# Statistics in the third buffer of scaled scores, and the value products of tiles 12 and 13 ahead of the first wo part, behind an attention loop

## The chip, the cores and the metric

The kernel runs on one core of a Trainium2 chip. The metric is device time in microseconds (us), the median of several executions. The engines are named as in the profile: PE multiplies matrices (PEld is its weight load), DVE, ACT and POOL do elementwise work, and SP issues DMA transfers. POOL also issues some.

## The reference, cut to what matters

One block: an adaptive layer norm, attention against a cached K and V, a second adaptive layer norm, and a mixer with an MLP. Everything is bf16 at the edges; x has 2048 rows of D = 640, there are 32 heads of 128, and 2048 cached keys.

```python
mod = (silu(c) @ w_mod).reshape(...)          # sa, ca, ga, sb, cb, gb
h = layernorm(x) * (1 + ca) + sa
q = (h @ wq)                                  # 32 heads of 128
p = softmax(q @ k_cache.T * 128 ** -0.5)
x = x + ga * ((p @ v_cache) @ wo)
h = layernorm(x) * (1 + cb) + sb
y = gelu(layernorm(h) @ w1)                   # quarters of its columns shifted by +1, -1, +2, -2 rows
x1 = h + shifted(y) @ w2
x = x + gb * (x1 + gelu(layernorm(x1) @ w3) @ w4)
```

So each row passes three more statistics (mean and variance over 640 columns) behind the attention: of x (level 0), of h (level 1) and of x1 (level 2).

## The kernel before

The rows are cut into NQT = 16 tiles of 128. The attention loop runs over NG = 512 steps s (head h, tile j). In a step, PE makes the scores (`qk`, L295), DVE scales them into one of three buffers of `negS` (buffer s % 3) and takes the row minimum (L583), ACT makes the exponentials into a ring (`Pb`, L596), and these are transposed, mostly by DMA (L226) and for some tiles on PE (`t_piece`, L257, with a copy out of the bank by ACT, L266, or DVE, L268). Some 8 to 11 steps later PE makes the value products (`pv`, L308) into two banks `O`; ACT copies a pair of tiles out (`of_copy`, L535); and POOL normalizes a group of four tiles (`rcp` L449, `norm` L456) into one of two halves of `On` and issues the store of that group to a scratch in DRAM (`o_scratch`, L463).

Behind the loop the order is written out by hand (L744 to L768). Left over from the loop are the last eight tiles of the last head: tiles 8 to 11 (steps NG - 8 to NG - 5), which were transposed by DMA, and tiles 12 to 15, which PE transposes (`t_all`). `pv2(g)` makes the value products of two tiles and their copy, and `norm4` normalizes and stores a group: 124 to 127 are the groups of tiles 0 to 3, 4 to 7, 8 to 11 and 12 to 15 of the last head.

`a_part(j, h0, h1, parts)` (L647) is the product of tile j's outputs with wo, for some heads and some columns (NC2: 512 and 128). It accumulates in one of two banks of `Sps`, (j + 1) % 2. Its outputs come transposed from `o_scratch`: `load_ot0` (L509) brings tiles 0 and 1, first 31 heads and then the last, into `hTx`; `load_ot(pr)` (L504) brings tiles 2 pr and 2 pr + 1, for odd pr into the first part of `negS` and for even pr into `hTx`. `load_xt` (L515) brings x. w1 (L769) and w2 (L770) are loaded behind all value products; w2 lies in `negS`, after the part that the outputs use.

In the loop over tiles from L773 on, `a_pe(i)` is tile i's wo product (tiles 0 and 1 are already made), `a_s1(i)` the gate, the sum with x (L659, L661) and the statistics of level 0, and `a_s2(i - 1)` the second norm (L667, L670) and the statistics of level 1. Then `nrm_of` (L682) and a transposing DMA `n_t` (L688) make the input of the mixer.

Statistics are in `stats_of`: two `bn_stats` (L635) and a `bn_aggr` (L637) on DVE; `rs_of` then makes (variance + eps) ** -0.5 on POOL (L628, L630), with the exponent from a small tile `mhalf`, which one memset (L771) fills. Before, all these small tiles lie over `On`, so L635 and the memset wait until `On` is free (ONK: every key of `On`).

Engines run their own instructions in program order; `Prog` puts a semaphore wait in front of an instruction for each key that it reads or writes and that another engine or a DMA wrote or read before.

Of the kernel before, what the change touches and what calls it, by code (L numbers as in the profile page):

```python
# [8 lines left out]
F32 = mybir.dt.float32  # L9
# [106 lines left out]
def bass_adaLN_cond__mha_block_cached__mixer_s_mlp__prompt_kernel(  # L116
    nc, A_x, A_k_cache, A_v_cache, A_wq, A_wo, B_x, B_w1, B_w2, B_w3, B_w4, c, w_mod, out,
):
    _, SQ, D = A_x.shape
    _, H, SK, DH = A_k_cache.shape  # L120
    FF = B_w3.shape[1]
    assert DH == 128 and D % 128 == 0 and SQ % 512 == 0 and SK == 2048
    KT = D // 128
# [8 lines left out]
    NG = H * NQT  # L132
# [5 lines left out]
    with ExitStack() as es:  # L138
# [11 lines left out]
        if True:  # L150
            with ExitStack() as es1:
# [7 lines left out]
                negS = sb1("negS", [128, 3, SK], F32)  # L159
# [5 lines left out]
                On = sb1("On", [128, 2, 4, 128], BF16)  # L165
# [35 lines left out]
                G = Prog(nc, es1, "a")  # L201
# [49 lines left out]
                def t_piece(g, r, q):  # L251
                    jb = bank(("t", g, r))

                    def f(t):
                        for z in range(4 * q, 4 * q + 4):
                            kt = 8 * r + z
                            ins = t.transpose(JBb[jb][:, z * 128:(z + 1) * 128], Pb[:, g % RPB, kt * 128:(kt + 1) * 128], ident[:])  # L257
                        return ins
                    G.op("tensor", f, r=[("Pb", g % RPB)], w=[("J", jb)])

                def t_evac(g, r):
                    jb = bank(("t", g, r))
                    dst = PTs[:, g % RPT, r * 8:(r + 1) * 8, :]
                    src = JBb[jb].rearrange("p (k q) -> p k q", k=8)
                    if not by_dve(g, r):
                        G.op("scalar", lambda a: a.copy(dst, src), r=[("J", jb)], w=[("PT", g % RPT, r)])  # L266
                    else:
                        G.op("vector", lambda v: v.tensor_copy(dst, src), r=[("J", jb)], w=[("PT", g % RPT, r)])  # L268
# [72 lines left out]
                if H > 1:  # L341
# [8 lines left out]
                     r=["id0"], w=["ident"])  # L350
# [3 lines left out]
                for k in range(KT):  # L354
                    G.op("gpsimd", lambda g, k=k: g.tensor_scalar(out=s_bc[:, k, :], in0=ones_f, scalar1=c_f[:, k:k + 1],
                                                                  scalar2=1.0, op0=ALU.mult, op1=ALU.mult),
                         r=["onesf", "cf"] + WRK, w=[("sbc", k)])
# [89 lines left out]
                def rcp(gr):  # L447
                    b = gr % 2
                    G.op("gpsimd", lambda g: g.tensor_tensor(  # L449
                        out=rl[:, 4 * b:4 * b + 4], in0=Of[:].rearrange("p a z d -> p (a z) d")[:, 4 * b:4 * b + 4, 128],  # L450
                        in1=mone, op=ALU.pow),
                         r=[("Of", 2 * b), ("Of", 2 * b + 1), "mone"], w=[("rl", b)])

                def norm(gr, z):
                    b = gr % 2
                    G.op("gpsimd", lambda g: g.tensor_scalar(  # L456
                        out=On[:, b, z, :], in0=Of[:, 2 * b + z // 2, z % 2, 0:128],
                        scalar1=rl[:, 4 * b + z:4 * b + z + 1], scalar2=1.0, op0=ALU.mult, op1=ALU.mult),
                        r=[("Of", 2 * b + z // 2), ("rl", b)], w=[("On", b, z)])
                    if z < 3:  # L460
                        return
                    hh, jj = divmod(4 * gr, NQT)
                    G.dma("gpsimd", lambda e: e.dma_start(  # L463
                        o_scr[jj // 2:jj // 2 + 2, :, hh].rearrange("a p z d -> p a (z d)"),
                        On[:, b].rearrange("p (a z) d -> p a (z d)", a=2)),
                        ("o", b), r=[("On", b, z) for z in range(4)], w=[("os", b), ("osd", jj // 4, hh)])
# [9 lines left out]
                negb = negS[:].rearrange("p r s -> p (r s)").bitcast(BF16)  # L476
# [10 lines left out]
                w4 = wof[:, KT * FF:KT * FF + NFT * D].rearrange("p (f n) -> p f n", f=NFT)  # L487
                ob = wof[:, KT * FF + NFT * D:KT * FF + (NFT + 2) * D].rearrange("p (b d) -> p b d", b=2)
                nrm = Of[:].rearrange("p a z d -> p (a z d)").bitcast(BF16)[:, 0:3 * D].rearrange("p (b d) -> p b d", b=3)
                sm = On[:].rearrange("p a z d -> p (a z d)").bitcast(F32)  # L490
                stt = sm[:, 0:NQT * 12].rearrange("p (t z) -> p t z", t=NQT)
                mvt = sm[:, 192:192 + 3 * NQT * 2].rearrange("p (l t z) -> p l t z", l=3, t=NQT)
                rst = sm[:, 288:288 + 3 * NQT].rearrange("p (l t) -> p l t", l=3)
# [1 line left out]
                mhalf = sm[:, 384:385]  # L495
# [4 lines left out]
                ONK = [("On", b, z) for b in range(2) for z in range(4)]  # L500
# [7 lines left out]
                def load_ot0(h0, h1):  # L508
                    G.dma("sync", lambda e: e.dma_start_transpose(  # L509
                        OTj[0][:, 2 * h0:2 * h1, :], o_scr[0, :, h0:h1].rearrange("q h z d -> q (h z d)")),  # L510
                        ("ot0", h0), r=[("osd", 0, hh) for hh in range(h0, h1)],
                        w=[("OT", 0)] + HTK if h0 == 0 else [("OTB", 0)])
# [9 lines left out]
                for g in range(NG - 8):  # L522
                    d = max(PVE, min(PVD, PVE + (NG - 12 - g) // 2))
# [15 lines left out]
                def norm4(gr):  # L539
                    rcp(gr)  # L540
                    for z in range(4):
                        norm(gr, z)

                for s in range(NG):
                    h, j = divmod(s, NQT)
# [5 lines left out]
                    if s == 3:  # L551
                        G.op("gpsimd", lambda g: g.tensor_scalar(
                            out=mod_bc[:, 2 * D:3 * D], in0=mod_bc[:, 2 * D:3 * D], scalar1=1.0, scalar2=1.0, op0=ALU.add, op1=ALU.mult),
                            r=[("mod", i) for i in range(len(MROW))], w=["mod"])
# [25 lines left out]
                    for half in range(2):  # L580
                        if s < NG:
# [6 lines left out]
                                r=[("S", half)], w=[("negS", s % 3), ("nmh", half, r8)])  # L588
# [3 lines left out]
                    if s < NG:  # L592
                        G.op("gpsimd", lambda g, r8=r8: g.tensor_scalar(  # L593
                            out=nm[:, r8:r8 + 1], in0=nm0[:, r8:r8 + 1], scalar1=nm1[:, r8:r8 + 1], scalar2=None, op0=ALU.min),
                            r=[("nmh", 0, r8), ("nmh", 1, r8)], w=[("nm", r8)])
                        G.op("scalar", lambda a, s=s, r8=r8: a.activation(  # L596
                            Pb[:, s % RPB, :], negS[:, s % 3, :], ACT.Exp, bias=nm[:, r8:r8 + 1], scale=-1.0),
                            r=[("negS", s % 3), ("nm", r8)], w=[("Pb", s % RPB)])
# [13 lines left out]
                    for g_ in NORMS.get(s, []):  # L612
                        gr, z = divmod(g_, 4)
# [13 lines left out]
                def rs_of(l, j):  # L627
                    G.op("gpsimd", lambda g: g.tensor_scalar(out=vet[:, l, j:j + 1], in0=mvt[:, l, j, 1:2], scalar1=float(EPS), scalar2=1.0,  # L628
                                                             op0=ALU.add, op1=ALU.mult), r=[("mvt", l, j)], w=[("vet", l, j)])
                    G.op("gpsimd", lambda g: g.tensor_tensor(out=rst[:, l, j:j + 1], in0=vet[:, l, j:j + 1], in1=mhalf, op=ALU.pow),  # L630
                         r=[("vet", l, j), "mhalf"], w=[("rst", l, j)])

                def stats_of(l, j, src, key):
                    for z in range(2):
                        G.op("vector", lambda v, z=z: v.bn_stats(stt[:, j, 6 * z:6 * z + 6], src[:, z * HD:(z + 1) * HD]),  # L635
                             r=[key], w=[("stt", j, z)] + ONK)
                    G.op("vector", lambda v: v.bn_aggr(mvt[:, l, j], stt[:, j, :]), r=[("stt", j, 0), ("stt", j, 1)], w=[("mvt", l, j)])  # L637
                    rs_of(l, j)

                def a_part(j, h0, h1, parts):  # L640
                    b = (j + 1) % 2
                    pr, z = divmod(j, 2)

                    def f(t):
                        for c0, cw in parts:
                            for hh in range(h0, h1):
                                ins = t.matmul(YB[b][:, c0:c0 + cw], OTj[pr % 2][:, 2 * hh + z, :], wo[:, hh, c0:c0 + cw],  # L647
                                               start=(hh == 0), stop=(hh == H - 1))
                        return ins
                    G.op("tensor", f, r=[("OTB", 0) if pr == 0 and h0 == H - 1 else ("OT", pr % 2)] + WOK, w=[("S", b)])  # L650
# [42 lines left out]
                for n in range(KT):  # L693
                    lst = []
                    p = 0
                    while p < 128:
# [8 lines left out]
                        p = pe_  # L705
# [27 lines left out]
                def t_all(g, r):  # L733
                    for q in range(2):
                        t_piece(g, r, q)
                    t_evac(g, r)

                def pv2(g):
                    for g_ in (g, g + 1):
                        for half in range(2):  # L740
                            pv(g_, half)
                    of_copy(g // 2)

                for g in (NG - 4, NG - 3):  # L744
                    for r in range(2):
                        t_all(g, r)
                norm4(H * 4 - 3)
                load_ot0(H - 1, H)
                a_part(0, 0, H // 2, NC2[0:1])
                for r in range(2):  # L750
                    t_all(NG - 2, r)
                a_part(0, H // 2, H - 1, NC2[0:1])
                for r in range(2):
                    t_all(NG - 1, r)
                pv2(NG - 4)
                a_part(0, 0, H - 1, NC2[1:2])
                pv2(NG - 2)
                norm4(H * 4 - 1)
# [9 lines left out]
                norm4(H * 4 - 2)  # L768
                G.dma("sync", lambda e: e.dma_start(w1, B_w1.rearrange("(k p) n -> p k n", p=128)), "w1", w=["w1"] + KVK)  # L769
                G.dma("sync", lambda e: e.dma_start(w2, B_w2.rearrange("(k p) n -> p k n", p=128)), "w2", w=["w2"] + NEG)  # L770
                G.op("gpsimd", lambda g: g.memset(mhalf, -0.5), w=["mhalf"] + ONK)  # L771

                for i in range(NQT + 1):  # L773
                    if i < NQT:
# [114 lines left out]
                for op_, in1, r_ in ((ALU.mult, mod_bc[:, 3 * D:4 * D], ["mod"]), (ALU.add, xt[:, NQT - 1], [("x1", NQT - 1)])):  # L889
                    G.op("gpsimd", lambda g, op_=op_, in1=in1: g.tensor_tensor(out=xb[:, NQT - 1], in0=xb[:, NQT - 1], in1=in1, op=op_),  # L890
                         r=r_ + [("xb", NQT - 1)], w=[("xb", NQT - 1), ("xg", NQT - 1)])
# [31 lines left out]
```

## Time and profile before

| | |
|---|---|
| time, median of 3 runs | 1604.11 us (1598.97 to 1604.65) |
| the profiled execution | 1605.5 us, span 1603.7 us |
| mean granted clock of PE | 0.994 |
| PE busy | 1511.8 us, 94% |
| DVE busy | 1397.1 us, 87% |
| ACT busy | 1269.4 us, 79% |
| POOL busy | 626.3 us, 39% |
| end of the last exponential | 1269.5 us |
| first wo part (L647) starts | 1270.1 us |
| last matmul of the wo products ends | 1428.9 us |

Times in what follows are us from the start of the span. The span is the profiled execution from its first to its last instruction; 1.8 us of the execution lie around it. A list of waits gives the engine, its line and who released it, and idle time in a timeline stands in square brackets. Everything up to about 1267 us is the same instructions before and after the change.

### The profile page before, as it was taken

Reading aid. Unit: us, or ns where it says so; the run is one execution under the profiler, and the core shown is the slowest. Engines: PE = TensorE matmul, PEld = TensorE weight load, DVE = VectorE, ACT = ScalarE, POOL = GpSimd, SP = SyncE. Lnnn points to the kernel's source line nnn. Section 1 sums busy time; section 2 is a strip of 40 time slices with the busy share of each in tenths; the row PEclk is TensorE's granted clock in tenths of the full one; section 3 lists DMA queues with packets and bytes.
Section 4 is the critical chain, followed back from the end, with each engine's and each line's share of the span. In section 5 each row is a group of like instructions: output and inputs, shape, how many; then the busy total and the mean of one; then the engine's idle time right before and its main releaser. Section 6 shows DMA issues by size and latency. Waiting matters only on the chain.

```text
span 1603.7 us, 34871 instructions
## 1 busy us (share of the span) xinstructions
PE 1511.8 (94%) x14119; PEld 956.1 (60%) x14119; DVE 1397.1 (87%) x2466; ACT 1269.4 (79%) x1114; POOL 626.3 (39%) x1396
## 2 busy tenths in 40 slices
PE   5899999999999999999999999999999889999999
PEld 3466666666666666666666666666666655554444
DVE  6999999999999999999999999999999637667424
ACT  4999999999999999999999999999999600034230
POOL 0144444444444444444444444444444433332100
PEclk9999999999999999999999999999999999999999
DMA  9999999999999999999999999999999987815100
GB/s 296 241 228 234 233 247 237 247 233 232 241 228 238 237 229 234 243 237 240 247 249 234 236 228 242 234 238 232 235 232 239 238 199 145 159 31 152 38 17 34
DMA packets 1183073, 337.27 MB, mean 210 GB/s; under 512 B 1163648, under 2 KB 1176896, under 8 KB 1182912
## 3 DMA queue, kind: packets, MB, share of 16 engines
q1 hardware_dynamic: 1176768, 318.26, 101.9%
q0 software_dynamic: 6144, 16.79, 3.1%
q8 instruction: 111, 1.82, 0.5%
q14 instruction: 50, 0.41, 0.1%
HBM read 43.48 MB, written 19.40 MB: 39 GB/s over the span
## 4 chain that ended last, share of the span: by engine, by line
ACT 32%; PE 21%; DMA 21%; DVE 17%; issue 8%; POOL 0%; ACTq 0%; DVEq 0%; POOLq 0%
ACT ring L596 26%; DMA ring<-ring 19%; DVE negS L583 15%; PE Sps L647 8%; PE Sps L845 4%; ACT ring L266 2%; ACT Of L535 2%; PE Oaug L829 2%; PE QPp L829 2%; ACT kv L248 1%; PE Sps L811 1%; PE PTp L308 1%; DVE ring L373 1%; PE Sps L295 1%; DMA hTx<-o_scratch 1%
## 5 line engine op out<-in xcount | busy, mean ns | idle before, releaser
L583 DVE TENSOR_SCALAR_CACHE_REDUCE negS<-Sps 128x1024 f32<-128x1024 f32 x1024 | 1179.2, 1221 | 35.8 <-PE Sps L295 17.7
L596 ACT ACTIVATE ring<-negS,small 128x2048 bf16<-128x2048 f32 x512 | 1008.4, 2019 | 37.9 <-DMA ring<-ring 29.7
L308 PEld LDWEIGHTS PTp<-kv,ring 128*128 128x128 bf16 x8192 | 558.8, 98 | 238.6 <-DMA ring<-ring 1.4
L295 PE MATMUL Sps<-kv 128*128 128x512 bf16 x2048 | 618.3, 384 | 50.5 <-DVE negS L583 42.8
L308 PE MATMUL PTp<-kv,ring 128*128 128x129 bf16 x8192 | 644.1, 220 | 0.4 <-DMA ring<-ring 0.4
L593 POOL TENSOR_SCALAR small<-small 128x1 f32<-128x1 f32 x512 | 145.9, 285 | 632.8 <-DVE negS L583 632.5
L295 PEld LDWEIGHTS Sps<-kv 128*128 128x128 bf16 x2048 | 125.9, 97 | 198.5 <-DVE negS L583 164.5
L456 POOL TENSOR_SCALAR On<-Of,small 128x128 bf16<-128x128 f32 x512 | 189.8, 371 | 13.2 <-DMA o_scratch<-On 0.3
L449 POOL TENSOR_TENSOR small<-Of,small 128x4 f32<-128x4 f32 x128 | 133.2, 1040 | 26.3 <-ACT Of L535 26.1
L241 PE MATMUL Oaug<-hTx,kv 128*128 128x512 bf16 x320 | 122.1, 386 | 11.2 <-ACT ring L266 8.3
L241 PE MATMUL QPp<-hTx,kv 128*128 128x512 bf16 x320 | 120.5, 381 | 2.6 <-ACT hTx L400 2.0
L463 POOL DMA_DIRECT2D o_scratch<-On x128 | 103.1, 806 | 40.8 <-POOL On L456 37.2
L535 ACT COPY Of<-PTp 128x259 f32<-128x259 f32 x256 | 97.1, 379 | 16.0 <-PE PTp L308 16.0
L727 ACT ACT_TABLE_LOAD x1 | 1.3, 1283 | 112.3 <-POOL hTx L778 112.3
L583 DVE DVE_READ_ACCUMULATOR negS<-Sps 128x1 f32 x1024 | 85.9, 84 | 0.0
L647 PE MATMUL Sps<-wo,negS 128*128 128x128 bf16 (+1 forms) x512 | 73.0, 305 | 5.4 <-DVE ring L659 5.4
L647 PE MATMUL Sps<-wo,hTx 128*128 128x512 bf16 (+1 forms) x512 | 70.7, 299 | 2.4 <-DMA hTx<-o_scratch 2.4
L628 POOL TENSOR_SCALAR On<-On 128x1 f32<-128x1 f32 x48 | 24.6, 512 | 118.2 <-DVE On L637 118.2
L862 DVE TENSOR_TENSOR ring<-Sps,ring 128x640 f32<-128x640 f32 x15 | 12.4, 824 | 65.5 <-PE Sps L845 65.5
L266 ACT COPY ring<-Oaug 128x1024 bf16<-128x1024 bf16 x64 | 65.5, 1024 | 4.7 <-PE Oaug L257 4.7
L647 PEld LDWEIGHTS Sps<-wo,negS 128*128 128x128 bf16 x512 | 40.2, 99 | 37.8 <-DVE ring L659 5.6
L647 PEld LDWEIGHTS Sps<-wo,hTx 128*128 128x128 bf16 x512 | 39.4, 98 | 32.2 <-DMA hTx<-o_scratch 2.6
(84 smaller groups left out, 975.5 us busy)
## 6 DMA issues: line engine op xcount, KB each, us to landing
kv<-in_A_v_cache_dram SPq DMA_DIRECT2D x32, 512.0 KB, 5.0
o_scratch<-On POOLq DMA_DIRECT2D x128, 128.0 KB, 5.2
ring<-in_A_x_dram SPq DMA_DIRECT2D x8, 640.0 KB, 6.0
kv<-in_A_wq_dram SPq DMA_DIRECT2D x32, 160.0 KB, 3.8
wo<-in_A_wo_dram SPq DMA_DIRECT2D x1, 5120.0 KB, 16.9
ring<-ring SPq DMA_TRANSPOSE x254, 7.2
ring<-in_w_mod_dram SPq DMA_DIRECT2D x1, 3200.0 KB, 14.2
out_dram<-wo SPq DMA_DIRECT2D x16, 160.0 KB, 1.8
```

The source lines that it names most:

```text
L241: G.op("tensor", lambda t: t.matmul(JB[jb], wq[:, hb, q, :], hT[:, q, cc * 512:(cc + 1) * 512], start=(q == 0), stop=(q == KT - 1)), r=[(" ...
L266: G.op("scalar", lambda a: a.copy(dst, src), r=[("J", jb)], w=[("PT", g % RPT, r)])
L295: ins = t.matmul(Sps[:, col:col + 512], QT[:, hb, j * 128:(j + 1) * 128], KTs[:, hb, col:col + 512], start=True, stop=True)
L308: ins = t.matmul(ob[:, 0:129], PTs[:, b, kt, :], Vaug[:, hb, kt, 0:129], start=(kt == 0), stop=(kt == NKT - 1))
L449: G.op("gpsimd", lambda g: g.tensor_tensor(out=rl[:, 4 * b:4 * b + 4], in0=Of[:].rearrange("p a z d -> p (a z) d")[:, 4 * b:4 * b + 4, 128 ...
L456: G.op("gpsimd", lambda g: g.tensor_scalar(out=On[:, b, z, :], in0=Of[:, 2 * b + z // 2, z % 2, 0:128], scalar1=rl[:, 4 * b + z:4 * b + z ...
L463: G.dma("gpsimd", lambda e: e.dma_start(o_scr[jj // 2:jj // 2 + 2, :, hh].rearrange("a p z d -> p a (z d)"), On[:, b].rearrange("p (a z) d ...
L535: G.op("scalar", lambda a: a.copy(Of[:, p % 4].rearrange("p z d -> p (z d)")[:, 0:259], PO[:, (p % 2) * 512:(p % 2) * 512 + 259]), r=[("O" ...
L583: G.op("vector", lambda v, half=half, s=s, r8=r8: v.tensor_scalar(out=negS[:, s % 3, half * 1024:(half + 1) * 1024], in0=Sps[:, half * 102 ...
L593: G.op("gpsimd", lambda g, r8=r8: g.tensor_scalar(out=nm[:, r8:r8 + 1], in0=nm0[:, r8:r8 + 1], scalar1=nm1[:, r8:r8 + 1], scalar2=None, op ...
L596: G.op("scalar", lambda a, s=s, r8=r8: a.activation(Pb[:, s % RPB, :], negS[:, s % 3, :], ACT.Exp, bias=nm[:, r8:r8 + 1], scale=-1.0), r=[ ...
L647: ins = t.matmul(YB[b][:, c0:c0 + cw], OTj[pr % 2][:, 2 * hh + z, :], wo[:, hh, c0:c0 + cw], start=(hh == 0), stop=(hh == H - 1))
```

## The change

The statistics' tiles move from `On` to the end of the third buffer of `negS`, after the part where w2 goes (elements 11392 to 12162 of 12288 in bf16). `bn_stats` now depends on `mhalf` and no longer on `On`; the memset of `mhalf` is placed ahead of `norm4` of group 125 and waits for the third buffer of `negS`. In the order behind the loop, the transposes of tile 14 and the value products of tiles 12 and 13 (`pv2(NG - 4)`) come ahead of the first wo part, and the transposes of tile 15 ahead of the second.

```diff
-                sm = On[:].rearrange("p a z d -> p (a z d)").bitcast(F32)
+                SM0 = 2 * H * 128 + KT * D
+                assert 2 * SK * 2 <= SM0 and SM0 + 770 <= 6 * SK
+                sm = negb[:, SM0:SM0 + 770].bitcast(F32)
...
                         G.op("vector", lambda v, z=z: v.bn_stats(stt[:, j, 6 * z:6 * z + 6], src[:, z * HD:(z + 1) * HD]),
-                             r=[key], w=[("stt", j, z)] + ONK)
+                             r=[key, "mhalf"], w=[("stt", j, z)])
...
                 for g in (NG - 4, NG - 3):
                     for r in range(2):
                         t_all(g, r)
+                G.op("gpsimd", lambda g: g.memset(mhalf, -0.5), w=["mhalf", ("negS", 2)])
                 norm4(H * 4 - 3)
                 load_ot0(H - 1, H)
+                for r in range(2):
+                    t_all(NG - 2, r)
+                pv2(NG - 4)
                 a_part(0, 0, H // 2, NC2[0:1])
                 for r in range(2):
-                    t_all(NG - 2, r)
+                    t_all(NG - 1, r)
                 a_part(0, H // 2, H - 1, NC2[0:1])
-                for r in range(2):
-                    t_all(NG - 1, r)
-                pv2(NG - 4)
                 a_part(0, 0, H - 1, NC2[1:2])
                 pv2(NG - 2)
                 norm4(H * 4 - 1)
...
                 G.dma("sync", lambda e: e.dma_start(w2, B_w2.rearrange("(k p) n -> p k n", p=128)), "w2", w=["w2"] + NEG)
-                G.op("gpsimd", lambda g: g.memset(mhalf, -0.5), w=["mhalf"] + ONK)
```

Behind these lines, unchanged: `load_xt(0)`, `load_ot(1)`, `load_xt(1)` to `load_xt(3)`, the wo product of tile 1 and the last head of tiles 0 and 1, `pv2(NG - 8)`, `pv2(NG - 6)` (tiles 8 to 11), `norm4` of group 126, and the loads of w1 and w2.

## The prediction

> **What bounds the kernel now.** I read the page first: PE is busy for 1511.8 of 1603.7 us, and the change touches only what follows the attention loop, so only gaps of PE behind the loop can pay. The list of waits between 1255 and 1332 us (engine, line, waited for: total, times, longest) names them:
>
> ```profile
> DVE On L635 <- POOL On L771: 14.5, 1, 14.5
> POOL On L771 <- DMA o_scratch<-On: 7.9, 1, 7.9
> PE Sps L647 <- DVE ring L659: 5.4, 1, 5.4
> PE Sps L647 <- DMA hTx<-o_scratch: 2.4, 1, 2.4
> ```
>
> PE has two gaps: 2.4 us before the first wo part, which waits for a load of outputs, and 5.4 us later, where DVE has yet to empty a bank of scores. The chain of waits (start us, us, what) shows what stands behind the second:
>
> ```profile
> 1284.24 8.96 PE Sps L647 x66
> 1293.20 3.75 PE PTp L308 x64
> ...
> 1300.29 8.66 DMA o_scratch<-On
> ...
> 1309.00 0.10 POOL On L771
> ...
> 1309.20 0.90 DVE On L635 x2
> ...
> 1310.33 0.70 DVE ring L659
> ```
>
> The statistics of tile 0 (L635) are written over the outputs' buffer On, so they wait until group 126 has been stored from it; the multiply of tile 1 (L659), queued behind them on DVE, frees the bank that PE wants for tile 3. Next, the timeline of PE and the stretches around the gap (us, us; busy time and count for PE, PEld, DVE, ACT, POOL; granted clock, DMA share, GB/s):
>
> ```profile
> 1311.07 11.30 PE L647 MATMUL Sps<-wo,negS 128*128 128x512 bf16 x64 [5.43 <-DVE ring L659]
> ```
>
> ```profile
> 1268.00:1272.00 4.00, 1.89 (x9) 0.90 (x10) 0.48 (x1) 1.54 (x1) 2.99 (x6) 1.00 1.25 274
> 1312.00:1314.00 2.00, 2.00 (x6) 0.66 (x5) 1.93 (x5) 0.00 (x0) 0.79 (x2) 0.50 1.07 242
> 1314.00:1316.00 2.00, 2.00 (x6) 0.76 (x5) 1.93 (x5) 0.00 (x0) 1.17 (x2) 0.50 0.00 0
> ```
>
> After the 5.4 us gap the granted clock is 0.50 until about 1316, and tile 3's 64 matmuls take 11.30 us. Tile 4 starts at 1322.21, 11.14 us after tile 3; undisturbed, the chain gives 8.69 us for 64 of them (at 1420.15). So the gap costs another 2.45 us. After the 2.4 us gap the clock stays 1.00. Last, what comes in next:
>
> ```profile
> 1296.97 0.37 SPq L769 DMA_DIRECT2D kv<-in_B_w_dram  x1
> 1297.39 0.53 SPq L770 DMA_DIRECT2D negS<-in_B_w_dram  x1
> 1297.96 14.19 SPq L504 DMA_TRANSPOSE hTx<-o_scratch  x1
> ```
>
> This L504 brings the outputs of tiles 4 and 5. The rows of L504 give 11.1/11.5/16.3 us to landing (least, median, most), and the look at its own issue gives it the 16.3: it lands at 1314.26. PE asks for it at 1322.21, so it is hidden today by 8 us. From 1311 to 1428.9 the chain is PE without a gap, and after that PE but for some 5 us of ACT at L727 near 1430 to 1437 and DVE's last 2 us; whatever moves tile 4 moves the end.
>
> **The value products (second part).** PE's work is the same; its order differs. Before: transposes of tiles 12 and 13 end at 1267.67, idle to 1270.11. After: tile 14's transposes stand here. Their exponentials end at 1267.38 (ACT: two from 1263.48, 3.90 us). Their banks are freed by DVE's copies of tile 13 (L268, 1267.19 and 1267.80, 0.69 and 0.68 us), so the halves (0.45 us each in the chain) run at 1267.95 and 1268.55, to 1269.00. The value products of tiles 12 and 13 need those same copies, so they follow at once: 1.87 us, to 1270.9. The load that PE waited for landed at 1270.06. Then, with the chain's pieces: 3.63 + 0.90 + 3.24 + 1.73 + 1.87 = 11.37 us (wo of 16 heads, transposes of tile 15, wo of 15 heads, wo's last 128 columns, products of 14 and 15), so tile 1's wo part starts at 1282.27 instead of 1284.24: 1.97 us gained of 2.44. ACT's copies of tile 14 now queue behind the last exponential (to 1269.54) and end at 1271.6; tile 15 wants the banks at 1274.5, so nobody waits. Behind them the copy of the products of 12 and 13 (L535, 0.37 us) ends at 1272; group 127, which wants it, waits for the products of 14 and 15 anyway. The stores of groups 127 and 126 (POOL, from 1287.59 and 1300.29) go out 2 us earlier; group 125's stays. Tile 2's wo part moves from 1296.96 to 1294.99, and its outputs (L504 at 1277.88, 14.7 us) landed at 1292.6.
>
> **The statistics (first part).** The memset (0.09 us, L771) goes ahead of group 125's normalization on POOL. It waits for the exponential of tile 13, done at 1265.4; POOL idles 1.55 us until 1267.72 there, so it is hidden, and behind it only group 125 would wait. The load of tiles 2 and 3 gains a wait on this memset on SP, met 11 us before its issue at 1277.88. Writing 6 numbers into negS in place of On has no row: nearest is L635 itself, 0.45 us each on On. I take no change; 0.1 us either way on four of them a tile leaves DVE at about 7.2 of 8.69 us a tile, so 0 on the path.
>
> DVE on the new timing: tile 0's L659 at 1290.9, L661, two L635 and L637 (0.82 + 0.82 + 0.89 + 0.21, with gaps 2.8), then tile 1's L659 frees the bank at 1294.5. PE wants it for tile 3 at 1294.99 + 8.69 = 1303.68: the 5.4 us wait and the half clock go. Now queued behind a wait: tile 0's L670 needs POOL's L630, which stands behind group 126's normalization and its DMA issue (1298.3 to 1299.1) and is done near 1300.3; DVE reaches tile 2's L659 by 1302.5, before PE offers it at 1303.68. Tile 4 could start at 1312.37.
>
> **What is late next.** The load of tiles 4 and 5. SP is free from 1295.87 (L769 waited 1.1 us, for the products of tiles 8 to 11, which will end at 1294.99), so w1, w2 and this load are issued at most 1.07 us earlier. The landing has two bounds: 1314.26 if DMA work sets it, 1313.2 if the issue does. DMA is busy 0.27 at 1294 to 1296, 0.54 to 1298, 0.95 to 1300 and over 1 afterwards, so about half of the advance falls into free time: 1313.7. PE then waits 1.3 us (under the 2.4 us that left the clock at 1.00) and tile 4 starts at 1313.75: 1322.21 - 1313.75 = 8.5 us gained. As terms: 1.97 + 5.43 + 2.45 - 1.35 (new wait) = 8.5. Next after that is the load of tiles 6 and 7: issue when tile 3 ends, 1312.4, plus 11.3, lands at 1323.8 for a start at 1331.1; covered.
>
> The profiled execution took 1605.5 us (span 1603.7 and 1.8 around it), 1.4 above the median of 1604.11. It becomes 1597.0; the same 8.5 off the median gives 1595.6.
>
> **Rivals.**
> A: the landing stays at 1314.26, and moving the products buys nothing. For: DMA share above 1 from 1300 to 1314. Gain 1322.21 - 1314.3 = 7.9; 1596.2. Chance 0.2.
> B: the load is hidden, since w1 and w2 finish earlier in DMA's idle time and the store of group 126 no longer falls into it (other L504 take 11.1 to 11.5 us). Gain 1322.21 - 1312.37 = 9.8; 1594.3. Chance 0.15.
> C: half clock at the first wo part. Three tiles' transposes now stand in a row in front of it. Price: one stretch at 0.50, 2.45 us by tile 3. The products of tiles 8 to 11 then end at 1297.4, w1 is issued 0.5 us later than now, and the load lands and tile 4 starts near 1314.8: gain 7.4, 1596.7. Against: from 1264.48 to 1270.11 PE already ran nothing but transposes and waits, and the clock was 1.00 from 1264 to 1272. Chance 0.06. [...]
> D: the change doesn't free DVE, because something else holds tile 0's statistics. Against: the chain has no other link. Only the 2 us of the second part remain: 1602.1. Chance 0.05.
> E, slower: statistics written beside what PE reads. PE takes weights from negS in eight wo tiles (512 matmuls), w2 as moving data (160) and half of the last weights (8 x 28 = 224), 896 in all. It decides from 8.5/896 = 9.5 ns each; at 20 ns it costs 17.9 us, 1613.5. No row has DVE writing in negS while PE reads it; but the two L647 groups, out of hTx and out of negS, differ only by 73.0 - 70.7 = 2.3 us, which the half clock explains, and DVE's writes are a few numbers a tile. Chance 0.04.
>
> **How the numbers follow.** The forecast keeps 0.5. About 0.5%, 8 us, is what a measurement of this kernel can tell from no change, and the forecast lies just over it: the runs shown spread over 1598.97 to 1604.65, so a median can move by 2 to 3 us. Of the forecast I count 0.7 as over the bound, of B nearly all, of A under half, of C a third: 0.35 + 0.14 + 0.09 + 0.02 = 0.6 faster; 0.04 slower; the rest, 0.36, within. The range is B less 3 us, 1591.3, to C plus 2.3, 1599.0, which leaves out D, E and the far ends of the spread. The forecast's own range, by its landing bounds (gain 7.9 to 9.0), is 1595.1 to 1596.2 without the spread.
>
> **What would show it.** Right: no wait of L635 on the memset; PE's idle before the first wo part about 0; tile 3's 64 matmuls in 8.7 us at clock 1.00; a wait of PE for the load of tiles 4 and 5 of 0 to 2 us; tile 4 starting near 1313.75. Wrong: PE idle over 3 us anywhere from 1265 to 1330, a clock under 1.00 there, the L647 or L811 means of negS risen by 10 ns, or that load landing after 1315.

## The result, and the profile after

The changed kernel takes 1597.34 us (median of 20 executions, 1590.56 to 1604.36), the kernel before 1606.94 (20 executions, 1598.97 to 1612.36): 9.6 us less by the medians. The ratio is 0.9934, with a 95% interval of 0.9918 to 0.9949, or 8 to 13 us; the predicted 8.5 lies at its near end, and the predicted time, 1595.6, 1.7 us under the median. The profiled execution has a span of 1594.3 us. The new lines move everything in the loop over tiles down by two: L504 is now L506, L647 is L649, L659 is L661.

The list of waits of the changed kernel over the same stretch as before, 1255 to 1332 us (engine, line, waited for: total, times, longest), with the rows of PE and of the statistics:

```profile
DVE ring L672 <- POOL negS L632: 3.4, 1, 3.4
...
PE Oaug L257 <- DVE ring L268: 1.4, 2, 1.0
...
PE Sps L649 <- DMA hTx<-o_scratch: 1.1, 1, 1.1
```

DVE no longer waits for the memset, nor PE for the bank. What is left for PE is 1.4 us among the transposes and 1.1 us at a load. The timeline of PE shows where (start us, us; idle time before in brackets):

```profile
1267.48 0.61 PE L257 MATMUL Oaug<-ident,ring 128*128 128x128 bf16 x8 [0.35 <-DVE ring L268]
1267.99 0.62 PE L257 MATMUL QPp<-ident,ring 128*128 128x128 bf16 x8
1268.45 2.04 PE L308 MATMUL PTp<-kv,ring 128*128 128x129 bf16 x32
1270.32 3.61 PE L649 MATMUL Sps<-wo,hTx 128*128 128x512 bf16 x16
...
1294.22 17.55 PE L649 MATMUL Sps<-wo,negS 128*128 128x512 bf16 x128
1312.84 12.54 PE L649 MATMUL Sps<-wo,hTx 128*128 128x512 bf16 x81 [1.08 <-DMA hTx<-o_scratch]
```

Tiles 2 and 3 now run as one block of 128 matmuls in 17.55 us, at most 8.8 us a tile. The load that tile 4 waits for is the one named, and the timeline of SP gives its issue:

```profile
1296.04 14.58 SPq L506 DMA_TRANSPOSE hTx<-o_scratch  x1
```

The load takes 16.75 us to land, until 1312.80, and tile 4 starts at 1312.84. And the clock (us, us; busy time and count of PE, PEld, DVE, ACT, POOL; granted clock, DMA share, GB/s): tile 3 runs in the first two of these stretches; the last two, which had the half clock before, now hold the start of tile 4.

```profile
1304.00:1306.00 2.00, 2.00 (x11) 0.94 (x10) 1.93 (x5) 0.00 (x0) 0.00 (x0) 1.00 1.05 208
1306.00:1308.00 2.00, 2.00 (x11) 0.91 (x10) 1.93 (x3) 0.00 (x0) 1.88 (x2) 1.00 1.23 231
...
1312.00:1314.00 2.00, 1.16 (x6) 0.57 (x7) 1.93 (x4) 0.00 (x0) 0.00 (x0) 1.00 0.65 142
1314.00:1316.00 2.00, 2.00 (x11) 0.91 (x10) 1.93 (x5) 0.00 (x0) 1.18 (x2) 1.00 0.96 198
```

From tile 4 to the end of the span it is 281.5 us in both profiles: all of the difference lies ahead of tile 4.

### The profile page after: what moved, and what is told of

The parts are those of the page before. It is cut to its first block, busy times and chain, and to the rows that moved or that the text cites. A ratio compares the mean times of both kernels' runs of the same rounds, so it can differ in the third digit from the quotient of the medians.

```text
span 1594.3 us, 34871 instructions
## 1 busy us (share of the span) xinstructions
PE 1506.9 (95%) x14119; PEld 955.5 (60%) x14119; DVE 1397.4 (88%) x2466; ACT 1269.2 (80%) x1114; POOL 626.6 (39%) x1396
## 4 chain that ended last, share of the span: by engine, by line
DVE 26%; ACT 24%; PE 20%; DMA 19%; issue 9%; SPq 0%; POOL 0%; ACTq 0%; DVEq 0%; POOLq 0%
DVE negS L585 24%; ACT ring L598 19%; DMA ring<-ring 17%; PE Sps L649 7%; PE Sps L847 4%; ACT ring L266 2%; PE Oaug L831 2%; PE QPp L831 2%; ACT Of L537 1%; PE Sps L813 1%; DMA hTx<-o_scratch 1%; PE Sps L295 1%; PE PTp L308 1%; ACT kv L248 1%; DVE ring L373 1%
## 5 line engine op out<-in xcount | busy, mean ns | idle before, releaser
L649 PE MATMUL Sps<-wo,hTx 128*128 128x512 bf16 (+1 forms) x512 | 70.5, 299 | 1.1 <-DMA hTx<-o_scratch 1.1
L630 POOL TENSOR_SCALAR negS<-negS 128x1 f32<-128x1 f32 x48 | 23.8, 496 | 119.5 <-DVE negS L639 119.3
L649 PE MATMUL Sps<-wo,negS 128*128 128x128 bf16 (+1 forms) x512 | 70.4, 299 | 0.0
L661 DVE TENSOR_TENSOR ring<-Sps,mod_bc 128x640 f32<-128x640 f32 x16 | 13.1, 821 | 52.2 <-PE Sps L649 52.2
L649 PEld LDWEIGHTS Sps<-wo,hTx 128*128 128x128 bf16 x512 | 39.5, 98 | 31.1 <-DMA hTx<-o_scratch 1.2
```

## The experiments

Spans differ by up to 32 us between profiles although the loop is the same in all: it ends anywhere from 1247 to 1268 us. So I compare the tail, from the first transpose of tile 12 to the end of the span. It is 339.2 us before and 330.4 in the changed kernel, 8.8 less. Some profiles lack the first matmul of a block: a block then shows 15 or 63 instead of 16 or 64. Its start is taken here from what released it (a load or DVE), 0.05 us behind that ("issue" in the chains of before and of the changed kernel), which puts it 0.22 us ahead of the first row at the full clock (a matmul, by the 3.45 us for 16 in the changed kernel's chain) and, by an estimate of twice that, up to 0.43 at the half clock. The runs e5, e6, e7 and e10 are single executions and have no interval of their own, and the profiles come from several chips.

| kernel | 16 matmuls of the first wo part | gap before tile 3 | tile 3 | wait at tile 4 | tail |
|---|---|---|---|---|---|
| before | 3.6 | 5.4 | 11.3 | 0 | 339.2 |
| before, once more (e10) | 5.1 | 4.6 | 11.7 | 0 | 340.4 |
| changed | 3.6 | 0 | 8.7 | 1.1 | 330.4 |
| changed, once more (e8) | 3.6 | 0 | 8.7 | 0.4 | 329.7 |
| part one alone (e1) | 5.3 | 0 | 8.7 | 0 | 332.9 |
| part two alone (e2) | 3.6 | 3.7 | 11.4 | 0 | 335.6 |
| changed, load first (e3; again, e9) | 3.6 | 0 | 8.7 | 0 | 329.2; 329.2 |
| before, matmuls in the gap (e4) | 5.3 | filled | 8.9 | 0 | 338.0 |
| part one, load first (e5) | 5.0 | 0 | 8.7 | 0 | 332.6 |
| before, transposes in the gap (e6) | 5.3 | filled | 8.9 | 0 | 340.2 |
| before, first gap filled (e7) | 3.6 | 6.0 | 11.4 | 0 | 340.0 |

**Part one alone.**

```diff
-                sm = On[:].rearrange("p a z d -> p (a z d)").bitcast(F32)
+                SM0 = 2 * H * 128 + KT * D
+                assert 2 * SK * 2 <= SM0 and SM0 + 770 <= 6 * SK
+                sm = negb[:, SM0:SM0 + 770].bitcast(F32)
...
-                             r=[key], w=[("stt", j, z)] + ONK)
+                             r=[key, "mhalf"], w=[("stt", j, z)])
...
+                G.op("gpsimd", lambda g: g.memset(mhalf, -0.5), w=["mhalf", ("negS", 2)])
                 norm4(H * 4 - 3)
...
-                G.op("gpsimd", lambda g: g.memset(mhalf, -0.5), w=["mhalf"] + ONK)
```

> Part one alone: the statistics in the third buffer, the order of the value products as before. Measure in the trace: the tail, from the first transpose of tile 12 to the end of the span, which is 339.2 us in the kernel before (1603.7 - 1264.5) and 330.4 in the changed kernel (1594.3 - 1263.9), 8.8 less. Theory (the gap of PE, 5.43, and the half clock behind it, 2.45, go with part one; the load of tiles 4 and 5 lands just as PE comes): tail shorter than before by 7.5 to 7.9 us, tile 3 in 8.7 us at clock 1.00, idle of 2.4 us before the first wo part still there, PE's wait for the load of tiles 4 and 5 between 0 and 0.4 us. Rival (part two carries more than a fifth of the gain, since the early products also bring the load forward): tail shorter by 6 or less. Time against before: 0.995.

Time: 0.995 (0.9926 to 0.9974). Tail 6.3 us shorter than before, where 7.5 to 7.9 was expected; all that was expected of tiles 2 to 4 came true, so the miss lies ahead of them. The timeline of PE and the stretch show it:

```profile
1265.85 5.31 PE L649 MATMUL Sps<-wo,hTx 128*128 128x512 bf16 x16 [2.50 <-DMA hTx<-o_scratch]
```

```profile
1266.00:1268.00 2.00, 2.00 (x6) 0.76 (x5) 0.00 (x0) 0.00 (x0) 1.10 (x2) 0.51 1.28 290
```

A wait of 2.44 us left the clock at 1.00 in the profile of before; here one of 2.50 us did not, and the first wo part took 5.3 us instead of 3.6. Without these 1.7 us part one gained 8.0.

**Part two alone.**

```diff
+                for r in range(2):
+                    t_all(NG - 2, r)
+                pv2(NG - 4)
                 a_part(0, 0, H // 2, NC2[0:1])
                 for r in range(2):
-                    t_all(NG - 2, r)
+                    t_all(NG - 1, r)
                 a_part(0, H // 2, H - 1, NC2[0:1])
-                for r in range(2):
-                    t_all(NG - 1, r)
-                pv2(NG - 4)
```

> Part two alone: the new order of the value products, the statistics still over the outputs' buffer. Theory: the idle before the first wo part goes, everything behind comes 2 us earlier, the store of group 126 too, and the gap before tile 3 (5.4 us) and the half clock behind it stay: tail shorter than before by 2.0 us. Rival (the load of group 126's store sets the gap's end at a fixed time, because DMA is full): the gap before tile 3 grows by what was gained, tail shorter by 0 to 1 us. Time against before: 0.999, not to be told from 1.

Time: 0.996 (0.9943 to 0.9978). Tail 3.6 us shorter, more than either theory had: the gap was 3.7 us, since the store of group 126 landed 6.9 us after its issue instead of 8.7. 1.97 + 1.7 makes the 3.6. The half clock behind the gap stayed:

```profile
1293.78 11.36 PE L647 MATMUL Sps<-wo,negS 128*128 128x512 bf16 x64 [3.74 <-DVE ring L659]
```

What makes that store take 6.9 us in e2, 8.7 in the profile of before and 9.2 in e7 is not settled. Where the statistics have left On, nobody on PE's path waits for it.

**The load of tiles 4 and 5 ahead of w1 and w2, in the changed kernel.**

```diff
+                load_ot(2)
                 G.dma("sync", lambda e: e.dma_start(w1, B_w1.rearrange("(k p) n -> p k n", p=128)), "w1", w=["w1"] + KVK)
...
-                        if i % 2 == 1 and (i + 3) // 2 < NQT // 2:
+                        if i % 2 == 1 and i > 1 and (i + 3) // 2 < NQT // 2:
```

> The changed kernel, with the load of the outputs of tiles 4 and 5 issued ahead of those of w1 and w2 (which are wanted 100 us later). Theory (PE's remaining wait of 1.08 us at tile 4 is that load queued behind w1 and w2): the load lands at 11 to 13 us from an issue near 1295, that is before 1308, the wait is gone, and the tail is 1.1 us shorter than in the changed kernel: 329.3, 9.9 less than before. Rival (the load shares DMA with w1 and w2 whatever the order, or the wait turns up at the next load): the tail stays at 330.4. Time against before: 0.993 to 0.994; from the changed kernel not to be told apart by times alone.

Time: 0.9938 (0.9914 to 0.9962). The tail is 329.2, 1.2 us under the changed kernel's, as expected. The timelines of SP and PE:

```profile
1278.51 11.18 SPq L506 DMA_TRANSPOSE hTx<-o_scratch  x1
1289.74 0.57 SPq L773 DMA_DIRECT2D kv<-in_B_w_dram  x1
```

```profile
1277.49 17.55 PE L649 MATMUL Sps<-wo,negS 128*128 128x512 bf16 x128
1294.88 17.55 PE L649 MATMUL Sps<-wo,hTx 128*128 128x512 bf16 x128
```

The load lands 13.2 us after its issue, at 1291.7, 3 us before PE wants it, and tiles 2 to 5 run without a gap. So the new wait was a place in the queue behind w1 and w2. Of the 4.4 us by which the load lands earlier than in the changed kernel, counted from the first transpose, 0.8 is the earlier issue and 3.6 the shorter time to landing (13.2 instead of 16.75 us), with w1 and w2 issued behind it, from 1289.74, instead of ahead.

**Matmuls in the gap of the kernel before.**

```diff
                         b = a_pe(i)
+                        if i == 2:
+                            def dummy(t):
+                                for _ in range(24):
+                                    ins = t.matmul(PO[:, 0:512], wo[:, 0, 0:128], wo[:, 0, 0:512], start=True, stop=True)
+                                return ins
+                            G.op("tensor", dummy, r=WOK, w=[("O", 0)])
```

> The kernel before, with 24 matmuls of 128x512 into a free bank between the wo products of tiles 2 and 3; their result is not used. They take 24 x 0.216 = 5.2 us of the 5.4 us gap, so DVE's release of the bank still sets when tile 3 starts. Theory (2.45 us of the cost of the gap is the clock that the idle PE loses): tile 3 starts as before, runs at clock 1.00 in 8.7 us instead of 11.1 to 11.3, and the tail is 2.4 us shorter than before: 336.8. Rival (tile 3 is slow for another reason, DMA or DVE at work on the same memory): tile 3 still takes 11 us, tail 339.2. Time against before: 0.998 to 0.999.

Time: 0.9988 (0.9967 to 1.001), not to be told from 1. In the timeline of PE, L779 is the added work:

```profile
1298.87 5.34 PE L779 MATMUL PTp<-wo 128*128 128x512 bf16 x24
1304.05 8.86 PE L647 MATMUL Sps<-wo,negS 128*128 128x512 bf16 x64
```

Tile 3 starts as late as before, within 0.4 us, and yet runs at full speed (8.86 us, the granted clock 1.00 from 1300 to 1312), with the same DMA and DVE work beside it: here the half clock was the price of idling, and by itself it was 2.45 us. The tail missed its expected 336.8 by 1.2, because the first wo part took 5.3 us again (+ 1.7), less 0.4 by which tile 3 started sooner.

**Part one, with the load first.** The edits of e1 and e3.

> Part one alone, with the load of tiles 4 and 5 ahead of w1 and w2. In part one alone that load landed 0.6 us before PE came. Theory (part two's worth is 1.97 us of PE's idle time, and the load only hid 1.1 of it in the changed kernel): this kernel's tail equals that of part one alone, 331.2 to 331.3 us where the first wo part (16 matmuls) takes 3.6 us, 332.9 where it takes 5.3, and is longer than that of the changed kernel with the load first (329.2) by 2.0 or 3.7. Rival (the order of the loads gains by itself, on any order of the products): tail of 330.2 or less with the first part at 3.6.

Tail 332.6, the first part 5.0: 3.5 us longer than the changed kernel with the load first. Of these 1.4 are the clock of the first part and 2.1 the order of the products, 1.97 by the prediction. Against part one alone the tail is shorter only by the clock (0.3), so the order of the loads gains nothing there. So part two is worth 2 us of idle time, plus the clock.

**Transposes in the gap of the kernel before.**

```diff
                         b = a_pe(i)
+                        if i == 2:
+                            def dummy(t):
+                                for z in range(128):
+                                    ins = t.transpose(PTp[:, (z % 8) * 128:(z % 8 + 1) * 128], wo[:, 0, 0:128], ident[:])
+                                return ins
+                            G.op("tensor", dummy, r=WOK, w=[("O", 0)])
```

> The kernel before, with 128 transposes of 128x128 on PE into a free bank between the wo products of tiles 2 and 3 (their result is not used); 128 x 0.056 = 7.1 us, which covers the gap of 5.4 us and 1.7 more. Theory (only idle PE loses its clock; transposes hold it like matmuls): tile 3 runs in 8.7 to 8.9 us at clock 1.00, starting 1.7 us later than before, tail 339.2 + 1.7 - 2.45 = 338.5 where the first wo part takes 3.6 us, 340.2 where 5.3. [...]

The timeline of PE and the stretch during the transposes:

```profile
1298.19 7.31 PE L779 MATMUL PTp<-ident,wo 128*128 128x128 bf16 x128
1305.55 8.64 PE L647 MATMUL Sps<-wo,negS 128*128 128x512 bf16 x63
```

```profile
1298.00:1302.00 4.00, 4.00 (x76) 4.00 (x74) 0.89 (x2) 0.00 (x0) 0.09 (x1) 1.00 1.25 276
```

128 transposes in a row took 0.057 us each at clock 1.00, and tile 3 ran at full speed behind them. Here transposes held a clock that was already full; whether they would raise a low one, no run shows. Tail 340.2, as expected with a first part of 5.3.

**The first gap filled with matmuls, in the kernel before.**

```diff
+                def dummy(t):
+                    for _ in range(11):
+                        ins = t.matmul(PO[:, 0:512], wo[:, 0, 0:128], wo[:, 0, 0:512], start=True, stop=True)
+                    return ins
+                G.op("tensor", dummy, r=WOK, w=[("O", 0)])
                 a_part(0, 0, H // 2, NC2[0:1])
```

> The kernel before, with 11 matmuls of 128x512 into a free bank between the transposes of tile 13 and the first wo part (2.4 us, their result is not used), in the 2.4 us in which PE waits for the load. Of three profiles with this order, the first wo part's 16 matmuls took 5.3 us in two (clock 0.50) and 3.6 us in one. Theory (the idle time among transposes is what costs the clock there, by chance of where it falls): 3.5 to 3.7 us here, clock 1.00; tail 339.2 to 339.4, as in the profile before that kept its clock. Rival (the slow first part comes from the load's transfers or from the outputs just written): 5.3 us here as well as in the two.

```profile
1260.11 2.32 PE L752 MATMUL PTp<-wo 128*128 128x512 bf16 x10
1262.72 3.63 PE L647 MATMUL Sps<-wo,hTx 128*128 128x512 bf16 x16 [0.29 <-DMA hTx<-o_scratch]
```

With PE kept at work the first part takes 3.6 us, though the load that it waits for is the same. This is one profile, and the kernel before gave 3.6 once unaided. The tail, 340.0, is 0.6 to 0.8 over the expected one, because the store of group 126 took 9.2 us and the gap was 6.0.

**The kernels once more.**

> The changed kernel once more, beside the next two on one chip. Theory (part two also takes away a half clock at the first wo part, which four of five profiles of the old order show and none of three of the new order): first wo part's 16 matmuls in 3.6 us, tail 330.4 within 0.6. Rival (the new order keeps its clock there by chance only): 4.8 to 5.3 us. Time against before: 0.993 to 0.995.

> The changed kernel with the load of tiles 4 and 5 first, once more. Theory: tail 329.2, 1.2 us under the changed kernel's, first wo part in 3.6 us; time 0.0007 of the whole under the changed kernel's, which the intervals (0.002 each) will not tell apart. Rival: tail as the changed kernel's.

> The kernel before once more, for its first wo part. Theory (the idle time of 2.4 to 2.7 us among transposes costs the clock in most executions): 16 matmuls in 4.8 to 5.3 us, tail 340.5 to 340.9. Rival (the profile of before is the rule): 3.6 us, tail 339.2.

The changed kernel: 0.9948 (0.9924 to 0.9972), tail 329.7, 0.1 below what was expected; with the load first: 0.9919 (0.9887 to 0.9951), tail 329.2, 0.5 under the changed kernel's where 1.2 was expected. The two intervals overlap, so the times cannot tell them apart; the tails can, by 0.5 to 1.2 us, which is PE's wait at tile 4. The kernel before has a tail of 340.4, 0.1 below what was expected; in the timeline of PE:

```profile
1274.36 4.69 PE L647 MATMUL Sps<-wo,hTx 128*128 128x512 bf16 x15 [2.99 <-DMA hTx<-o_scratch]
```

With the first matmul, which is missing from this row and is counted at 0.43 us, the 16 took 5.1 us, and the 15 of the row took 4.69 where the same 15 took 3.40 in e8: that is a half clock again. Of six profiles with the old order and nothing added in front of the first wo part (before, e1, e4, e5, e6, e10), five show it there; of five with the new order (changed, e2, e3, e8, e9), none.

## Why the prediction was right

**The value products, 1.97 us: right.** Counted from the first transpose of tile 12, tile 2's wo part starts at 30.3 us instead of 32.3. The store of group 126 goes out only 1.5 us earlier, not 2, but nobody on PE's path waits for it.

**The statistics, 5.43 + 2.45 us: right.** Part one alone removed both, and e4 gave the second by itself. The statistics' new wait is met early, DVE's 3.4 us wait for POOL (L672) ends in time, as predicted, and writing beside what PE reads cost nothing here: L649 out of negS takes 299 ns in the mean, out of hTx 299, and L813 (L811 before) 299 as before. E has fallen, and D with it. Two readings in the prediction were off without harm: DVE's 7.2 us are of each 10 us and not of each tile (a tile takes 6.3 of its 8.69 us), and ACT at L727 is 3.0 us of the chain, not 5.

**The new wait, 1.35 us: the mechanism right, the size a little high.** It was 1.1 and 0.4 us in two profiles. Counted from the first transpose, the load was issued 1.4 us earlier (1.0 in e8), where at most 1.07 was allowed: SP itself came free 0.4 us earlier. It landed 0.9 us earlier (1.7 in e8); the bounds had 0 to 1.07. A has fallen, since the landing moved; B came near in e8, but only e3 hides the load.

**The step that was incomplete: the clock at the first wo part.** "After the 2.4 us gap the clock stays 1.00" was true of that one profile, and I took it for the rule. In most profiles of the old order the gap does cost the clock: over the six the excess of the first part over 3.6 us is 0, 1.7, 1.7, 1.4, 1.7 and 1.5, in the mean 1.3. Part two takes this away as well. So the sum is 8.5 + 1.3 + 0.3 to 1.0 (the smaller wait) = 10.1 to 10.8, inside the measured 8 to 13; and the mean tail of the two profiles of the kernel before is 9.8 us above that of the two of the changed kernel. It explains why both the ratio and the medians lie above 8.5. That the predicted time came within 1.7 us of the measured one is partly luck: the median of three that it was taken off was 2.8 us under that of the 20, which more than made up for the missing 1.1 us of gain.

What decides whether the gap tips the clock, these runs do not show: the wait of 2.44 us in the profile of before left it at 1.00, and one of 2.47 us in e4 halved it. How long it stayed down can be read. The stretches of e4 around the first gap and those of e10 around the second (columns as for the stretches above):

```profile
1260.00:1262.00 2.00, 0.17 (x1) 0.11 (x2) 0.16 (x1) 1.08 (x1) 1.73 (x5) 1.00 1.22 242
1262.00:1264.00 2.00, 2.00 (x8) 0.78 (x7) 0.00 (x0) 0.00 (x0) 0.81 (x1) 0.77 1.27 290
1264.00:1266.00 2.00, 2.00 (x6) 0.73 (x5) 0.00 (x0) 0.00 (x0) 0.00 (x0) 0.50 1.24 308
1266.00:1268.00 2.00, 2.00 (x21) 1.33 (x20) 0.00 (x0) 0.37 (x1) 0.00 (x0) 0.87 1.27 290
```

```profile
1310.00:1314.00 4.00, 0.94 (x17) 0.77 (x14) 0.32 (x1) 0.00 (x0) 0.09 (x1) 1.00 1.02 226
1314.00:1316.00 2.00, 0.05 (x1) 0.18 (x3) 1.93 (x5) 0.00 (x0) 0.77 (x2) 0.63 1.28 290
1316.00:1318.00 2.00, 2.00 (x5) 0.70 (x5) 1.93 (x5) 0.00 (x0) 0.39 (x1) 0.50 1.19 270
1318.00:1320.00 2.00, 2.00 (x6) 0.76 (x5) 1.93 (x4) 0.00 (x0) 1.53 (x2) 0.50 0.00 0
1320.00:1322.00 2.00, 2.00 (x7) 0.75 (x6) 1.90 (x5) 0.00 (x0) 0.74 (x2) 0.67 0.00 0
```

If each stretch is taken as part 1.00 and part 0.50, that is an estimate of 3.4 us of half clock in e4 (0.92 + 2.00 + 0.52) and 6.8 in e10 (1.48 + 4.00 + 1.32); in the profile of before the granted clock is 0.50 from 1309.20 to 1316.03, for 6.83 us, in which PE was busy for 4.96. Half of PE's work in that time comes to the measured price: 3.4 / 2 = 1.7 us in e4, and 4.96 / 2 = 2.5 at tile 3 of the kernel before, where 2.45 was measured. The new order leaves waits of 1.0 and 0.35 us in front of the first wo part. In its five profiles that part takes 3.6 us each time, in five of six of the old order 5.0 to 5.3; I do not take that for chance.

Rival C named the right effect at the right place, but for the wrong kernel, by the wrong cause and at 2.45 instead of up to 1.7 us: it is the old order that loses its clock there, by idling (with the gap filled, in e7, the part took 3.6 us), and the new one that keeps it. Transposes in a row did not lower the clock in these runs: the 128 of e6 ran for 7.31 us, and from 1298 to 1302 the granted clock was 1.00.

## What to carry to other kernels

A short wait of PE costs more than its length where it tips the clock (here 1.4 to 1.7 us on top of one of 2.4 to 2.7), and whether it does can differ between executions: look at the same gap in several profiles before calling its clock safe (this one kept it in one of six). Small tiles laid over a buffer inherit that buffer's last transfer (here a wait of 14.5 us for DVE); laying them over one that was free long before takes the transfer off the path. When work moves earlier, the next limit can be a place in a queue (here 0.5 to 1.2 us of the tail): put what is wanted first ahead of the bulk loads that are wanted a hundred us later.

## What was unexpected of the hardware

A gap of 2.4 to 2.7 us of PE, with 1.0 us of idle time shortly before, halved the granted clock in five of six profiles and cost 1.4 to 1.7 us; in the sixth the clock stayed at 1.00. Gaps of 3.7 to 6.0 us halved it in all four profiles in which nothing filled them (before, e2, e7, e10) and cost 2.4 to 2.9; behind waits of 1.1 us (changed) and 0.4 us (e8) the wo products ran at full speed, in the changed kernel at clock 1.00. 128 transposes in a row kept a full clock at 1.00 (e6), as 24 matmuls did (e4). And a 128 KB store of POOL's queue took 6.9 us (e2) to land and 9.2 (e7) while loads and DMA transposes were under way, and 8.7 and 7.8 us in two profiles of the same kernel.
